# Attention and feed-forward in one kernel: first quad's k and v loaded in three pieces, first batch's q loaded in attention order

## The chip, the cores and the metric

The kernel runs on one core of a Trainium2 chip. The core has five engines that run their own instruction queues in order: TensorE (PE, matmuls; its weight loads are listed as PEld), VectorE (DVE), ScalarE (ACT), GpSimd (POOL) and SyncE (SP), which here issues all the transfers. The metric is the device time of one execution in microseconds (us); the median of three is compared.

## The reference

A linear attention with a feature map, for 8 batches, 8 heads, 576 tokens and head size 64, followed by a feed-forward layer with exact Gelu on its 4608 rows of 512:

```python
def phi(x):
    proj = np.einsum('bhsd,df->bhsf', x, w_phi)
    proj = proj - np.max(np.abs(proj), axis=-1, keepdims=True)
    return np.concatenate([np.exp(proj), np.exp(-proj)], axis=-1)
q_p, k_p = (phi(q), phi(k))
kv = np.einsum('bhsf,bhsd->bhfd', k_p, v)
z = np.sum(k_p, axis=2)
num = np.einsum('bhsf,bhfd->bhsd', q_p, kv)
den = np.einsum('bhsf,bhf->bhs', q_p, z)[..., None] + 1e-06
x = num / den            # then transposed to (tokens, heads * 64)
h = x @ w_in             # 512 to 2048
g = 0.5 * h * (1.0 + erf(h / sqrt(2)))
out = g @ w_out          # 2048 to 512
```

All of it is in float32; w_phi has 128 features.

## The kernel before, in words

**The plan.** The kernel does not issue its instructions as it goes through its loops. Each step is put down as an operation (`Plan.op`, L79) with an engine, an assumed duration, the buffers that it reads and writes, and a rank. `Plan.order` (L105 to L230) then plays the whole kernel through on assumed clocks: at each step it takes, for each engine, the operations that could start first and of those the one with the lowest rank, gives it a start and an end, and frees buffers. `emit` (L232) issues everything in the order of the planned starts. On the chip each engine follows that order and waits by semaphores; the planned times themselves aren't enforced. An operation can be given an earliest planned start with `plan.since`: weight tile n is not loaded before 3.996 x n us (WPACE, L345 and L349), nothing of the feed-forward is planned before TF = 90 us (L622). The plan knows a duration for each kind of operation, hops between engines, TensorE's two clock rates, and a model of the transfers (L204 to L207). It assumes that VectorE and GpSimd do not disturb each other.

**The attention.** `attention(b, rank)` (L519) does a batch: two quads of four heads each. `k_quad` (L366) loads a quad's k (`kt`, 128 x 1152) and v (`vt`, 128 x 18 x 65, the last column ones) with one transfer each (L373, L375), and goes through five units of nine 128-token chunks: projection on TensorE into `pk`, absolute maximum on DVE (`mx`, L404), subtraction on DVE, two exponentials on ACT into `ek` (L408), and sums with v on TensorE into `kv`, copied to `kvn`. `q_pair` (L434) does two heads in two halves of 288 tokens: load `qt` (L443), project into `pq`, copy to `pc` on ACT, absolute maximum over partitions by an all-reduce on POOL (`mb`, L460), subtraction on DVE (`pc`, L311 through a helper), exponentials on ACT (`ef`, L466), and a matmul with `kvn` into `pn`. Results go to DRAM (`x_d`, `d_d`); `quotients` (L508) inverts the denominators. Matmuls are all recorded at L287, elementwise DVE steps at L311, copies at L305.

The operations of batch 0 have ranks from -200 upward in the order in which the code names them. In `q_pair` the load of q, its projection, copy, all-reduce and subtraction of batch 0 get a rank lower by EARLY = 37.5 (L436), so they come ahead of k and v of the same batch. Batch 1 has ranks from -180 (EPACE), the later ones have due times. Some buffers: two each of `kt`, `vt`, `qt`, `pc` and `ef`, one `mb`; the first two batches (EB = 2) use the two `ph` banks for `pq`, `pp` and `po` in turn for `pk`.

**The weights.** `split_weight` (L317) loads each of 32 weight tiles (128 x 512 of 64-bit words, `raw_i` and `raw_o`) and makes two float32r parts of it: one step on ACT, four on DVE (L327 to L333), a cast on ACT, a subtraction on DVE. 

**The feed-forward.** `block` (L539) takes 256 tokens: loads `xr` and `rb` (L552, L556), multiplies and splits them on DVE, and then for eight pairs of 128 columns of the middle layer does matmuls into `ph`, two Gelus on ACT (L582, L583), a subtraction on DVE (`gl`) and matmuls into `po`. There are 18 blocks.

**The start.** A memset on DVE, one small activation, and four matmuls on zeros (`spin`, WARM = 4) stand at the head of TensorE's queue while the first transfers run.

Of the kernel before, what the change touches and what calls it, by code (L numbers as in the profile page):

```python
# [24 lines left out]
NF = 128  # L25
# [29 lines left out]
class Op:  # L55
    __slots__ = ("eng", "cost", "fn", "bufs", "rank", "table", "late", "deps", "users", "wait", "ready", "start", "end", "n", "names", "nbytes", "duty", "kind")


class Plan:
# [18 lines left out]

    def op(self, eng, cost, fn, r=(), w=(), also=(), rank=0.0, table=None, late=0.0, kb=0, duty=1.0, kind="f"):  # L79
        o = Op()  # L80
        o.eng, o.cost, o.fn, o.rank, o.table, o.late, o.n = eng, cost, fn, rank, table, late, len(self.ops)
        o.users, o.ready, o.nbytes, o.duty, o.kind = [], self.since, kb, duty, kind
        deps = set()
        for b in r:
            deps.update(b.writers)
        for b in w:
            deps.update(b.writers)
            deps.update(b.readers)
        for b in r:
# [12 lines left out]
        self.ops.append(o)
        return o

    def order(self, bias):  # L105
# [53 lines left out]
        while len(done) < n:  # L159
# [91 lines left out]
def act(n, psum=False):  # L251
    return (n / 1.2 + (51 if psum else 93)) / 1e3
# [15 lines left out]
def fused_kernel(ctx: ExitStack, tc: tile.TileContext, qT, kT, va, w_st, w_in, w_out, out):  # L268
# [40 lines left out]
    def tt(eng, cost, dst, a, b, o, r, w, **kw):  # L309
        e = {"dve": nc.vector, "pool": nc.gpsimd}[eng]  # L310
        op(eng, cost, lambda: e.tensor_tensor(out=dst(), in0=a(), in1=b(), op=o), r=r, w=w, **kw)  # L311
# [54 lines left out]
    def k_quad(b, g, kvs, rank):  # L366
        def k():
            return dict(rank=next(rank))
# [3 lines left out]
        kt = sb["kt"]([P, KC * P], F32, f"kt_{nm}")  # L372
        op("sp", 0.06, lambda: nc.sync.dma_start(out=kt(), in_=kT[b, g]), w=[kt], kb=590, **k())  # L373
        vt = sb["vt"]([P, 18, D + 1], F32, f"vt_{nm}")
        op("sp", 0.06, lambda: nc.sync.dma_start(out=vt(), in_=va[b, g]), w=[vt], kb=600, **k())  # L375
        kv = [None, None]
# [8 lines left out]
        for u, (p, cs) in enumerate(units):  # L385
            n = len(cs)
            mx = sb["mx"]([P, 2, n], F32, f"mx_{nm}_{u}")
            x = ps[EARLY_PK[turn[0] % len(EARLY_PK)] if b < EB else "pp"]([P, 2, 512], F32, f"pk_{nm}_{u}")
# [10 lines left out]
            def proj(x=x, cs=cs):  # L399
                return [mm(x()[:, j, i * NF : (i + 1) * NF], lhsT=kt()[64 * j : 64 * j + 64, c * P : (c + 1) * P], rhs=wst()[64 * j : 64 * j + 64],  # L400
                           start=True, stop=True) for i, c in enumerate(cs) for j in range(2)]

            op("pe", n * PAIR_K, proj, r=[kt, wst], w=[x], also=[mx, *e], kind="k", **k())
            op("dve", dve(256 * n, True), lambda xs=xs, mx=mx: nc.vector.tensor_reduce(  # L404
                out=mx(), in_=xs(), axis=AX.X, op=ALU.max, apply_absolute_value=True), r=[x], w=[mx], **k())
            tt("dve", dve(256 * n, True), xs, xs, lambda mx=mx, n=n: mx().unsqueeze(3).to_broadcast([P, 2, n, NF]), ALU.subtract, [x, mx], [x], **k())
            for s in (1, 0):
                op("act", act(256 * n, True), lambda xs=xs, es=es, s=s: nc.scalar.activation(  # L408
                    es[s](), xs(), AF.Exp, scale=1.0 - 2.0 * s), r=[x], w=[e[s]], table="exp", **k())
            for pp in (0, 1) if p is None else (p,):  # L410
# [6 lines left out]
                for i, c in enumerate(cs):  # L417
# [10 lines left out]

                    op("pe", 4 * PAIR_V, sums, r=[*e, vt] + ([] if fresh and i == 0 else [acc]), w=[acc], kind="v", **k())
                if last_u:  # L430
# [108 lines left out]
    def block(j, rank):  # L539
# [25 lines left out]
        for u in range(NU):  # L565
# [17 lines left out]
            op("act", act(2 * TB, True) + 0.037, lambda ph=ph: nc.scalar.activation(ph(), ph(), AF.Gelu), r=[ph], w=[ph], table="gelu", rank=URGE + rk)  # L583
            tt("dve", dve(2 * TB, True), gl, ph, lambda gh=gh: gh().bitcast(F32), ALU.subtract, [ph, gh], [gl], rank=URGE + rk)
            for i in range(2):
# [64 lines left out]
LINGER = 3.0  # L650
# [49 lines left out]
```

## Time and profile before

| what | before |
|---|---|
| time, median of three executions | 1153.76 us (1150.57 to 1153.86) |
| the profiled execution's own time | 1153.51 us |
| its span in the trace | 1151.7 us |
| granted TensorE clock, mean of the span | 0.991 of full |
| busy: PE / DVE / ACT / POOL | 1111.6 / 483.5 / 588.9 / 318.2 us |
| TensorE instructions | 9096 matmuls |

How to read it: the profile lists, by engine, how long instructions ran, and for idle time which engine or transfer released it. A timeline row has start and duration in us, the engine, the line, the operation, what it writes and reads, and in brackets the idle time ahead of it with its releaser. In a row of groups the number after the bar is the busy time of the group, then the mean in ns. The chain of work that ended last is followed back from the last instruction. A busy TensorE is not one at its peak, since matmuls are pipelined.

### The profile page before, as it was taken

Reading aid. Unit: us, or ns where it says so; the run is one execution under the profiler, and the core shown is the slowest. Engines: PE = TensorE matmul, PEld = TensorE weight load, DVE = VectorE, ACT = ScalarE, POOL = GpSimd, SP = SyncE. Lnnn points to the kernel's source line nnn. Section 1 sums busy time; section 2 is a strip of 40 time slices with the busy share of each in tenths; the row PEclk is TensorE's granted clock in tenths of the full one; section 3 lists DMA queues with packets and bytes.
Section 4 is the critical chain, followed back from the end, with each engine's and each line's share of the span. In section 5 each row is a group of like instructions: output and inputs, shape, how many; then the busy total and the mean of one; then the engine's idle time right before and its main releaser. Section 6 shows DMA issues by size and latency. Waiting matters only on the chain.

```text
span 1151.7 us, 21761 instructions
## 1 busy us (share of the span) xinstructions
PE 1111.6 (97%) x9096; PEld 914.0 (79%) x9096; DVE 483.5 (42%) x807; ACT 588.9 (51%) x979; POOL 318.2 (28%) x116
## 2 busy tenths in 40 slices
PE   7887899999999999999999999999999999999998
PEld 4544677787787788788878778789898998989997
DVE  5999796344443534444354444432112212122010
ACT  5877586666684776658476675632121222122121
POOL 3323026345452635445263534430000000000000
PEclk8999999999999999999999999999999999999999
DMA  7667631313212041312213121112012021010000
GB/s 264 200 203 239 185 92 53 98 58 108 63 58 83 29 111 34 123 63 70 72 31 113 33 63 37 58 31 56 11 46 55 1 55 39 18 38 19 1 19 19
DMA packets 73939, 84.92 MB, mean 74 GB/s; under 512 B 23968, under 2 KB 60992, under 8 KB 73840
## 3 DMA queue, kind: packets, MB, share of 16 engines
q1 hardware_dynamic: 73840, 83.52, 24.3%
q8 instruction: 71, 1.16, 0.4%
q14 instruction: 28, 0.23, 0.1%
HBM read 64.32 MB, written 19.17 MB: 72 GB/s over the span
## 4 chain that ended last, share of the span: by engine, by line
PE 85%; DVE 7%; DMA 3%; ACT 2%; issue 1%; SPq 1%; POOL 0%; ACTq 0%; DVEq 0%; POOLq 0%
PE po L287 34%; PE ph L287 34%; PE kv L287 6%; PE pn L287 5%; PE pk L287 3%; PE pq L287 3%; DMA dc<-d_d 1%; DVE mx L404 1%; DVE pk L311 1%; DMA vt<-in_va_dram 1%; ACT ek L408 1%; DVE wt_o L331 1%; PE spin L287 1%; DMA x_d<-xo 1%; DVE w_i L311 0%
## 5 line engine op out<-in xcount | busy, mean ns | idle before, releaser
L287 PE MATMUL ph<-xh,w_i 128*128 128x256 f32 x2304 | 429.3, 282 | 0.0
L287 PEld LDWEIGHTS ph<-xh,w_i 128*128 128x128 f32 x2304 | 359.7, 188 | 13.5 <-issue 5.4
L287 PE MATMUL po<-w_o,gh 128*128 128x512 f32 x1152 | 366.9, 400 | 0.0
L287 PE MATMUL ph<-xl,w_i 128*128 128x256 f32 x1152 | 321.2, 279 | 0.0
L311 DVE TENSOR_TENSOR gl<-ph,gh 128x512 fp32r<-128x512 f32 x144 | 99.4, 690 | 386.5 <-ACT ph L583 385.7
L287 PEld LDWEIGHTS po<-w_o,gh 128*128 128x128 f32 x1152 | 207.5, 188 | 56.8 <-issue 9.9
L287 PE MATMUL po<-w_o,gl 128*128 128x512 f32 x576 | 227.8, 395 | 4.2 <-DVE gl L311 4.2
L460 POOL PARTITION_ALL_REDUCE mb<-pc x64 | 142.2, 2222 | 303.6 <-ACT pc L305 258.1
L582 ACT ACTIVATE gh<-ph 128x512 fp32r<-128x512 f32 x144 | 86.3, 599 | 272.6 <-PE ph L287 272.0
L287 PEld LDWEIGHTS ph<-xl,w_i 128*128 128x128 f32 x1152 | 216.5, 188 | 3.3
L495 POOL PARTITION_ALL_REDUCE db<-un x48 | 176.9, 3686 | 140.8 <-DVE un L492 136.5
L287 PEld LDWEIGHTS po<-w_o,gl 128*128 128x128 f32 x576 | 108.4, 188 | 31.1 <-DVE gl L311 5.8
L287 PEld LDWEIGHTS kv<-vt,ek 128*64 128x64 f32 (+1 forms) x2560 | 86.3, 141 | 41.6 <-ACT ek L408 18.0
L287 PE MATMUL pn<-ef,kvn 128*64 128x288 f32 (+1 forms) x512 | 98.8, 427 | 13.2 <-ACT xo L305 13.1
L287 PE MATMUL kv<-vt,ek 128*64 128x65 f32 (+1 forms) x2560 | 98.4, 229 | 13.3 <-ACT ek L408 11.7
L408 ACT ACTIVATE ek<-pk 128x512 f32<-128x512 f32 (+1 forms) x160 | 80.0, 553 | 41.4 <-DVE pk L311 40.6
L466 ACT ACTIVATE ef<-pc 128x576 f32<-128x576 f32 x128 | 83.1, 684 | 24.0 <-DVE pc L311 23.5
L583 ACT ACTIVATE ph<-ph 128x512 f32<-128x512 f32 x144 | 85.5, 594 | 0.0
L311 DVE TENSOR_TENSOR pc<-pc,mb 128x576 f32<-128x576 f32 x64 | 50.5, 790 | 83.1 <-POOL mb L460 83.1
L582 ACT ACT_TABLE_LOAD x55 | 70.6, 1283 | 19.6 <-PE ph L287 18.9
L404 DVE TENSOR_REDUCE mx<-pk 128x4 f32<-128x512 f32 (+1 forms) x80 | 50.5, 633 | 70.9 <-PE pk L287 70.9
L287 PEld LDWEIGHTS pn<-ef,kvn 128*64 128x64 f32 (+1 forms) x512 | 39.3, 138 | 45.4 <-ACT xo L305 17.1
(41 smaller groups left out, 702.3 us busy)
## 6 DMA issues: line engine op xcount, KB each, us to landing
vt<-in_va_dram SPq DMA_DIRECT2D x16, 585.0 KB
qt<-in_qT_dram SPq DMA_DIRECT2D x64, 144.0 KB
kt<-in_kT_dram SPq DMA_DIRECT2D x16, 576.0 KB
out_dram<-ob SPq DMA_DIRECT2D x36, 256.0 KB
raw_i<-in_w_in_dram SPq DMA_DIRECT2D x16, 512.0 KB
raw_o<-in_w_out_dram SPq DMA_DIRECT2D x16, 512.0 KB
x_d<-xo SPq DMA_DIRECT2D x48, 144.0 KB
x_d<-xo SPq DMA_DIRECT2D x32, 72.0 KB
```

Source lines behind the costliest of these rows:

```text
L287: return tc.keep_in_program_order(nc.tensor.matmul(*a, **kw))
L311: op(eng, cost, lambda: e.tensor_tensor(out=dst(), in0=a(), in1=b(), op=o), r=r, w=w, **kw)
L331: op("dve", dve(512), lambda: v.scalar_tensor_tensor(out=t(), in0=low(), scalar=29, in1=t(), op0=ALU.logical_shift_right, op1=ALU.bitwise_ ...
L404: op("dve", dve(256 * n, True), lambda xs=xs, mx=mx: nc.vector.tensor_reduce(out=mx(), in_=xs(), axis=AX.X, op=ALU.max, apply_absolute_val ...
L408: op("act", act(256 * n, True), lambda xs=xs, es=es, s=s: nc.scalar.activation(es[s](), xs(), AF.Exp, scale=1.0 - 2.0 * s), r=[x], w=[e[s] ...
L460: op("pool", 2.2, lambda mb=mb, pc=pc: nc.gpsimd.partition_all_reduce(mb(), pc(), P, bass_isa.ReduceOp.absmax), r=[pc], w=[mb], **k(1))
L466: op("act", act(2 * HS), lambda ef=ef, pc=pc, s=s: nc.scalar.activation(ef()[:, s], pc(), AF.Exp, scale=1.0 - 2.0 * s), r=[pc], w=[ef], ta ...
L495: op("pool", 3.7, lambda db=db, un=un: nc.gpsimd.partition_all_reduce(db(), un(), P, bass_isa.ReduceOp.add), r=[un], w=[db], **k())
L582: op("act", act(2 * TB, True) + 0.016, lambda gh=gh, ph=ph: nc.scalar.activation(gh(), ph(), AF.Gelu), r=[ph], w=[gh], table="gelu", rank= ...
L583: op("act", act(2 * TB, True) + 0.037, lambda ph=ph: nc.scalar.activation(ph(), ph(), AF.Gelu), r=[ph], w=[ph], table="gelu", rank=URGE + rk)
```

## The change

Three things are different in what is built:

1. k and v of batch 0's first quad are each loaded by three transfers (chunks 0 to 1, 2 to 4 and 5 to 8), k and v in turn. Each piece is a buffer of its own to the plan, and a unit's projection and sums depend on the piece that holds their chunks. All other quads keep one transfer each.
2. EARLY goes from 37.5 to 0, so the q steps of batch 0 have their ranks in the order of the code: behind k and v of their quad.
3. The planner charges a VectorE operation 0.9 us more (BLOCKED) where it overlaps a GpSimd operation by more than 0.3 us, once for each GpSimd operation. The operations marked `psum=True` (the maxima and subtractions of k, and the Gelu subtraction) are exempt. No instruction is added by this.

The tile `mx` is twice as wide, and its first half is used. A branch for `b < KB` is never taken, since KB is 0; `plan.since = HOLD2` sets the 0.0 that stood there.

```diff
-    def op(self, eng, cost, fn, r=(), w=(), also=(), rank=0.0, table=None, late=0.0, kb=0, duty=1.0, kind="f"):
+    def op(self, eng, cost, fn, r=(), w=(), also=(), rank=0.0, table=None, late=0.0, kb=0, duty=1.0, kind="f", psum=False):
...
+        taken = []
...
+            if o.eng == "dve" and not o.psum:
+                for span in taken[-4:]:
+                    if t < span[1] - 0.3 and t + cost > span[0] + 0.3 and not span[2]:
+                        span[2] = True
+                        cost += BLOCKED
+            if o.eng == "pool":
+                taken.append([t, t + cost, False])
...
         kt = sb["kt"]([P, KC * P], F32, f"kt_{nm}")
-        op("sp", 0.06, lambda: nc.sync.dma_start(out=kt(), in_=kT[b, g]), w=[kt], kb=590, **k())
         vt = sb["vt"]([P, 18, D + 1], F32, f"vt_{nm}")
-        op("sp", 0.06, lambda: nc.sync.dma_start(out=vt(), in_=va[b, g]), w=[vt], kb=600, **k())
+
+        kp, vp = {}, {}
+        for cut in ((0, 2), (2, 5), (5, KC)) if b == 0 and g < PIECES else ((0, KC),):
+            c0, c1 = cut
+            part, vpart = (Buf(plan, None, None) for _ in range(2))
+            op("sp", 0.06, lambda c0=c0, c1=c1: nc.sync.dma_start(out=kt()[:, c0 * P : c1 * P], in_=kT[b, g, :, c0 * P : c1 * P]),
+               w=[part], also=[kt], kb=65.6 * (c1 - c0), **k())
+            op("sp", 0.06, lambda c0=c0, c1=c1: nc.sync.dma_start(out=vt()[:, 2 * c0 : 2 * c1], in_=va[b, g, :, 2 * c0 : 2 * c1]),
+               w=[vpart], also=[vt], kb=66.6 * (c1 - c0), **k())
+            for c in range(c0, c1):
+                kp[c], vp[c] = part, vpart
...
-            mx = sb["mx"]([P, 2, n], F32, f"mx_{nm}_{u}")
+            mx = sb["mx"]([P, 2, 2 * n], F32, f"mx_{nm}_{u}")
...
-            op("pe", n * PAIR_K, proj, r=[kt, wst], w=[x], also=[mx, *e], kind="k", **k())
+            op("pe", n * PAIR_K, proj, r=[kp[cs[0]], wst], w=[x], also=[kt, mx, *e], kind="k", **k())
...
-                    op("pe", 4 * PAIR_V, sums, r=[*e, vt] + ([] if fresh and i == 0 else [acc]), w=[acc], kind="v", **k())
+                    op("pe", 4 * PAIR_V, sums, r=[*e, vp[c]] + ([] if fresh and i == 0 else [acc]), w=[acc], also=[vt], kind="v", **k())
...
-EARLY = 37.5
+EARLY = 0.0
...
+BLOCKED = 0.9
+HOLD2 = 0.0
...
+KB = 0
...
+PIECES = 1
```

More of the change, by code (lines that the diff above doesn't have):

```diff
@@ L55 @@
 class Op:
-    __slots__ = ("eng", "cost", "fn", "bufs", "rank", "table", "late", "deps", "users", "wait", "ready", "start", "end", "n", "names", "nbytes", "duty", "kind")
+    __slots__ = ("eng", "cost", "fn", "bufs", "rank", "table", "late", "deps", "users", "wait", "ready", "start", "end", "n", "names", "nbytes", "duty", "kind", "psum")
 class Plan:
@@ L77, in pool @@
         return lambda shape, dt, name: Buf(self, tag, lambda: pool.tile(shape, dt, tag=tag, name=name, bufs=bufs))
-    def op(self, eng, cost, fn, r=(), w=(), also=(), rank=0.0, table=None, late=0.0, kb=0, duty=1.0, kind="f"):
+    def op(self, eng, cost, fn, r=(), w=(), also=(), rank=0.0, table=None, late=0.0, kb=0, duty=1.0, kind="f", psum=False):
         o = Op()
         o.eng, o.cost, o.fn, o.rank, o.table, o.late, o.n = eng, cost, fn, rank, table, late, len(self.ops)
-        o.users, o.ready, o.nbytes, o.duty, o.kind = [], self.since, kb, duty, kind
+        o.users, o.ready, o.nbytes, o.duty, o.kind, o.psum = [], self.since, kb, duty, kind, psum
         deps = set()
@@ L401, in proj @@
                            start=True, stop=True) for i, c in enumerate(cs) for j in range(2)]
-            op("pe", n * PAIR_K, proj, r=[kt, wst], w=[x], also=[mx, *e], kind="k", **k())
+            op("pe", n * PAIR_K, proj, r=[kp[cs[0]], wst], w=[x], also=[kt, mx, *e], kind="k", **k())
             op("dve", dve(256 * n, True), lambda xs=xs, mx=mx: nc.vector.tensor_reduce(
-                out=mx(), in_=xs(), axis=AX.X, op=ALU.max, apply_absolute_value=True), r=[x], w=[mx], **k())
-            tt("dve", dve(256 * n, True), xs, xs, lambda mx=mx, n=n: mx().unsqueeze(3).to_broadcast([P, 2, n, NF]), ALU.subtract, [x, mx], [x], **k())
-            for s in (1, 0):
+                out=mx()[:, 0].rearrange("p (j i) -> p j i", j=2), in_=xs(), axis=AX.X, op=ALU.max, apply_absolute_value=True), r=[x], w=[mx], psum=True, **k())
+            if b < KB:
+                op("dve", 0.09, lambda mx=mx: nc.vector.tensor_scalar(
+                    out=mx()[:, 1], in0=mx()[:, 0], scalar1=-1.0, scalar2=None, op0=ALU.mult), r=[mx], w=[mx], **k())
+                for s in (1, 0):
+                    for j in range(2):
+                        for i in range(n):
+                            op("act", act(NF, True), lambda xs=xs, es=es, s=s, j=j, i=i, n=n, mx=mx: nc.scalar.activation(
+                                es[s]()[:, j, i], xs()[:, j, i], AF.Exp, scale=1.0 - 2.0 * s, bias=mx()[:, 1 - s, j * n + i : j * n + i + 1]),
+                               r=[x, mx], w=[e[s]], table="exp", **k())
+            else:
+                tt("dve", dve(256 * n, True), xs, xs, lambda mx=mx, n=n: mx()[:, 0].rearrange("p (j i) -> p j i", j=2).unsqueeze(3).to_broadcast(
+                    [P, 2, n, NF]), ALU.subtract, [x, mx], [x], psum=True, **k())
+            for s in (1, 0) if b >= KB else ():
                 op("act", act(256 * n, True), lambda xs=xs, es=es, s=s: nc.scalar.activation(
@@ L583, in block @@
             op("act", act(2 * TB, True) + 0.037, lambda ph=ph: nc.scalar.activation(ph(), ph(), AF.Gelu), r=[ph], w=[ph], table="gelu", rank=URGE + rk)
-            tt("dve", dve(2 * TB, True), gl, ph, lambda gh=gh: gh().bitcast(F32), ALU.subtract, [ph, gh], [gl], rank=URGE + rk)
+            tt("dve", dve(2 * TB, True), gl, ph, lambda gh=gh: gh().bitcast(F32), ALU.subtract, [ph, gh], [gl], rank=URGE + rk, psum=True)
             for i in range(2):
@@ L619, in fused_kernel @@
             continue
+        plan.since = HOLD2
         r0 = T0 + (b - 1) * AT - LEAD
```

## The prediction

> **What bounds the kernel now.** I read the page first: busy time of each engine, the slices, and the chain that ended last.
>
> ```profile
> span 1151.7 us, 21761 instructions
> PE 1111.6 (97%) x9096; PEld 914.0 (79%) x9096; DVE 483.5 (42%) x807; ACT 588.9 (51%) x979; POOL 318.2 (28%) x116
> PE   7887899999999999999999999999999999999998
> DVE  5999796344443534444354444432112212122010
> PE 85%; DVE 7%; DMA 3%; ACT 2%; issue 1%; SPq 1%; POOL 0%; ACTq 0%; DVEq 0%; POOLq 0%
> ```
>
> TensorE (PE) carries 85% of the chain. Only the first six slices or so, some 180 us, show it below nine tenths, and in those VectorE (DVE) is the busy engine. So I took the view of stretches, 40 us each; its columns are length, busy time of PE, weight load, DVE, ACT and POOL, then the granted clock, DMA share and GB/s.
>
> ```profile
> 0.00:40.00 40.00, 31.58 (x304) 19.59 (x304) 26.09 (x43) 23.81 (x51) 12.79 (x10) 0.91 0.71 246
> 40.00:80.00 40.00, 32.12 (x372) 20.16 (x372) 37.73 (x68) 30.44 (x67) 9.90 (x5) 0.91 0.68 203
> 80.00:120.00 40.00, 30.57 (x327) 18.12 (x324) 36.73 (x58) 32.10 (x71) 14.37 (x6) 0.96 0.75 233
> 120.00:160.00 40.00, 36.21 (x349) 29.65 (x347) 34.94 (x65) 26.88 (x45) 2.14 (x1) 0.99 0.54 152
> 160.00:200.00 40.00, 36.24 (x289) 28.09 (x288) 32.47 (x50) 27.57 (x43) 22.80 (x7) 0.96 0.20 55
> 200.00:240.00 40.00, 40.00 (x380) 32.27 (x378) 16.55 (x28) 27.33 (x42) 17.39 (x7) 1.00 0.28 84
> 320.00:360.00 40.00, 38.55 (x348) 31.51 (x347) 16.94 (x31) 24.10 (x37) 17.16 (x6) 1.00 0.23 64
> 720.00:760.00 40.00, 39.58 (x275) 31.81 (x275) 20.07 (x28) 23.83 (x36) 20.84 (x8) 1.00 0.22 59
> ```
>
> From 200 us on PE has no gap, but for 1.45 us in one of these stretches and 0.42 in another. Before 200 it is idle for 8.42 + 7.88 + 9.43 + 3.79 + 3.76 = 33.3 us. The change leaves the number of matmuls alone, so it can gain only in this head: a microsecond of PE idle that goes there comes off the end, one for one. From 40 to 120 us DVE is busy 74.5 of 80 us (the splitting of weights, and the attention). There an idle or wasted microsecond of DVE is what costs PE.
>
> **Part one, the pieces of k and v.** The start of PE, from its timeline, and the first two stretches of 5 us:
>
> ```profile
> 2.27 6.47 PE L287 MATMUL spin<-idle 128*128 128x512 f32 x8 [2.27 <-ACT idle L292]
> 8.67 0.76 PE L287 MATMUL pq<-qt,wst 64*128 64x288 f32 x4
> 9.26 1.06 PE L287 MATMUL pk<-wst,kt 64*128 64x128 f32 x16
> 10.15 0.81 PE L287 MATMUL pq<-qt,wst 64*128 64x288 f32 x4
> 13.18 2.14 PE L287 MATMUL kv<-vt,ek 128*64 128x65 f32 x64 [2.23 <-ACT ek L408]
> 0.00:5.00 5.00, 2.73 (x4) 1.19 (x5) 0.48 (x1) 1.49 (x2) 0.19 (x4) 1.00 0.55 163
> 5.00:10.00 5.00, 5.00 (x24) 2.57 (x24) 0.09 (x1) 0.55 (x2) 0.00 (x0) 1.00 1.01 392
> ```
>
> The warm-up matmuls (spin) hold PE until 8.74 us, and pq and pk follow with no wait for a transfer. By 5 us 163 x 5 = 815 KB have moved, then 392 KB in each microsecond. In the new order the first quad's k and v (590 + 600 KB in the planner's figures), w_st (66) and two q tiles (2 x 147) are 1550 KB: all landed, as an estimate, at 5 + 735/392 = 6.9 us, before the spin ends. So k in pieces is there earlier and nothing can use it: **gain 0**, whether or not a reader waits for one piece or all three. Four more issues on SP cost nothing as long as the engines of the DMA have work queued, which the share of 1.01 says. Without the cover of the spin, the worth would be the time between the first piece and the last, bounded by 1190/392 = 3.0 us.
>
> The Trainium skill, DMA: Bandwidth & Descriptors, section Bandwidth, speaks against pieces: its table has 138 GB/s for a 64 KB transfer and 341 for 1 MB, and asks for a MiB at a time. By that an estimate for the six pieces, 1190 KB at 138 GB/s, is 8.6 us, q would land after the spin ends, the next part's second term would be lost, and the result would be 1149.6. The trace has transfers of 147 to 600 KB queued back to back at 392 GB/s, which does not bear it out.
>
> **Part two, q in the order of the attention.** Today four pq matmuls go ahead of the first pk. Putting k first starts pk at 8.67 instead of 9.26, and with it the whole DVE stream, by 9.26 - 8.67 = **-0.6 us**; DVE bounds what follows, so I count it whole. Then the DVE and POOL timelines:
>
> ```profile
> 9.91 0.69 DVE L404 TENSOR_REDUCE mx<-pk 128x4 f32<-128x512 f32 x1 [8.53 <-PE pk L287]
> 12.57 0.75 DVE L311 TENSOR_TENSOR pc<-pc,mb 128x576 f32<-128x576 f32 x1
> 15.67 0.76 DVE L311 TENSOR_TENSOR pc<-pc,mb 128x576 f32<-128x576 f32 x1 [2.35 <-POOL mb L460]
> 10.25 2.14 POOL L460 PARTITION_ALL_REDUCE mb<-pc  x1 [9.82 <-ACT pc L305]
> 13.49 2.14 POOL L460 PARTITION_ALL_REDUCE mb<-pc  x1 [1.10 <-DVE pc L311]
> ```
>
> DVE stands still for 2.35 us at 13.3 because the second q subtraction is next in its queue and its all-reduce isn't done; the first quad's later units are behind it. With q after k, units of k fill that place. But the four q halves then come after, each with 2.14 us of all-reduce in front of a DVE instruction, so part of the wait may come back. Bounds 0 and -2.35, and +2.35 if a second such wait arises; I take half, **-1.2 us**, since weight splitting is at hand to fill by then.
>
> **Part three, the planner's new cost.** BLOCKED is the far-reaching edit: the planner now adds 0.9 us, once per POOL instruction, to a DVE instruction on SBUF that overlaps it. No instruction changes, but the order of every queue is worked out anew. Is the charge real? The groups of 0 to 130 us:
>
> ```profile
> L311 DVE TENSOR_TENSOR w_i<-wt_i,w_i 128x512 fp32r<-128x512 f32 x12 | 10.6, 880 | 1.6 <-ACT w_i L305 1.4
> L331 DVE SCALAR_TENSOR_TENSOR wt_i<-raw_i,wt_i 128x512 uint32<-128x512 uint32 x12 | 9.2, 770 | 0.2
> L333 DVE SCALAR_TENSOR_TENSOR wt_o<-raw_o,wt_o 128x512 uint32<-128x512 uint32 x11 | 8.4, 771 | 0.1
> L311 DVE TENSOR_TENSOR w_o<-wt_o,w_o 128x512 fp32r<-128x512 f32 x10 | 8.1, 829 | 1.5 <-ACT w_o L305 1.5
> L331 DVE SCALAR_TENSOR_TENSOR wt_o<-raw_o,wt_o 128x512 uint32<-128x512 uint32 x11 | 7.4, 684 | 0.1
> L327 DVE TENSOR_SCALAR wt_o<-wt_o 128x512 f32<-128x512 f32 x11 | 7.3, 671 | 0.2 <-ACT wt_o L326 0.2
> L329 DVE TENSOR_SCALAR wt_i<-wt_i 128x512 uint32<-128x512 uint32 x12 | 5.0, 422 | 0.1
> ```
>
> Against 684 ns for the same tile with two inputs and 422 with one, the others are long by 12 x 0.196 + 12 x 0.086 + 11 x 0.087 + 10 x 0.145 + 11 x 0.249 = 8.5 us, over the 16 all-reduces of two batches: about half a microsecond each that today's plan doesn't know of. The plan must then run ahead of the chip, and SP's timeline shows it where the code pins a plan time:
>
> ```profile
> 38.62 0.36 SPq L323 DMA_DIRECT2D raw_i<-in_w_in_dram  x1
> 67.35 0.36 SPq L323 DMA_DIRECT2D raw_o<-in_w_out_dram  x1
> 101.12 1.30 SPq L552 DMA_DIRECT2D xr<-x_d  x1
> 106.56 0.60 SPq L323 DMA_DIRECT2D raw_i<-in_w_in_dram  x1
> ```
>
> Counted from 0, these are weight loads 9, 15 and 24, and the first load of the feed-forward. The plan pins them at 3.996 x n or later and at TF = 90, so 36.0, 59.9, 95.9 and 90.0: the chip is late by 2.7, 7.4, 10.7 and 11.1 us. With some 16 x 0.9 = 14.4 us charged at most, the new plan keeps pace or lags a little, so weights and feed-forward loads stand some 10 us earlier in the queues against the attention of batches 1 and 2. What PE could gain from feed-forward work 10 us earlier:
>
> ```profile
> 116.04 1.19 PE L287 MATMUL pn<-ef,kvn 128*65 128x288 f32 x4 [2.92 <-ACT xo L305]
> 117.59 1.13 PE L287 MATMUL kv<-vt,ek 128*64 128x65 f32 x16 [0.37 <-ACT ek L408]
> 123.86 0.49 PE L287 MATMUL ph<-xh,w_i 128*128 128x256 f32 x1
> ```
>
> The first ph would start near 114 instead of 123.86 and fill these two gaps: 2.92 + 0.37 = **-3.3 us**. Bounds: nothing if DVE, being full, only trades one kind of work for another; at best these and the 7.55 us that PE idles from 120 to 200, -10.8 us; and above nothing, +5.9, the third rival's price. I take the gaps, the row where the moved work lands. After 200 us a new order has 1.87 us to win and as much to lose as it likes; I count 0.
>
> **The sum.** 0 - 0.6 - 1.2 - 3.3 = -5.1 us. The profiled execution took 1153.51 us (span 1151.7, 1.8 around it), 0.25 below the median of 1153.76; 1153.5 - 5.1 = **1148.4 us**. A measurement of this kernel tells about 0.3%, 3.5 us, from no change, so this would be seen as faster.
>
> **Rivals.** *Nothing to see:* DVE at 37.73 and 36.73 of 40 us is full whatever the order, so earlier feed-forward work takes its DVE time from the attention, PE loses there what it gains, and the waits for all-reduces come back. Only the earlier start stays: 1153.5 - 0.6 = 1152.9. For it speaks that the DVE work is the same to the instruction; against it, that a feed-forward group gives PE far more work for each DVE instruction than a weight or k does.
>
> *Slower, weights before attention:* the 10.7 us of lateness at load 24 are 10.7/4.0 = 2.7 weight tiles that the new plan puts ahead of attention work. A tile takes DVE 2 x 0.42 + 3 x 0.69 = 2.9 us, so attention is put off by 7.8 us of DVE, while no feed-forward matmul is ready before about 114. PE, busy 30.57 of 40 us then, loses 7.8 x 0.76 = 5.9 us: 1153.5 - 0.6 + 5.9 = 1158.8. It decides if PE's idle time from 40 to 120 us, now 17.3, comes to over 20. For it: T0, LEAD and WPACE stay as they were for the old plan. Against: the attention of batches 0 and 1 has the lower ranks, and the weights get what it leaves.
>
> *The change doesn't do what it says:* if the pieces only landed together, nothing would differ, as part one found.
>
> **The numbers.** Forecast (1142.7 to 1150.2, from the terms' far ends: all of the gaps and 5 us of the idle time behind them) 0.50; nothing to see 0.28; slower 0.22, of which about half lies within 4 us of no change. The range that leaves out 2 in 10: 1142 to 1157.5. Faster by over 0.3% 0.50, within 0.28, slower 0.22.
>
> **What would show it.** Part one: the spin still ends at 8.7, pk starts right behind it, kt and vt unwaited for. Part two: first DVE reduce near 9.3, no 2.35 us wait for mb before 16. Part three: weight load 24 near 97 to 100, the first xr load near 91 to 93, first ph near 114, PE idle before 200 us at 28 instead of 33.3. It is wrong if the first ph comes earlier and the idle total stays (first rival), if PE idles over 20 us from 40 to 120 (second), or if gaps open after 200 us.

## The result and the profile after

The changed kernel took 1161.62 us (median of 6, 1158.80 to 1164.28), the kernel before, on the same chip, 1153.33 us (median of 6, 1149.72 to 1153.90). The ratio is 1.0067, with a 95% interval of 1.0047 to 1.0087: slower by about two thirds of a per cent, where I forecast a gain of 5 us. The profiled execution took 1164.28 us (span 1162.5, mean granted clock 0.987 of full).

From the page of the changed kernel, the same lines as of before (span, busy time, slices of PE and of DVE, the chain by engine):

```profile
span 1162.5 us, 21746 instructions
PE 1121.1 (96%) x9096; PEld 921.7 (79%) x9096; DVE 503.8 (43%) x807; ACT 590.3 (51%) x981; POOL 320.0 (28%) x116
PE   8887898999999999999999999999999999999998
DVE  6997799353554535334543546352212112121110
PE 80%; DVE 8%; ACT 4%; DMA 3%; POOL 2%; issue 2%; SPq 1%; ACTq 0%; DVEq 0%; POOLq 0%
```

The second line holds the surprise. PE executes the same 9096 matmuls and is busy for 1121.1 us instead of 1111.6. So of the 10.8 us by which the span grew, 9.5 are matmuls that take longer, and 1.3 are idle time of PE (1162.5 - 1121.1 = 41.4 us against 40.1). Of the 9.5, 2.4 fall in the first 200 us (PE busy 169.2 us against 166.7), the other 7.1 behind them. The stretches of 40 us in the changed kernel:

```profile
0.00:40.00 40.00, 33.23 (x382) 21.05 (x382) 28.52 (x48) 27.43 (x60) 11.68 (x9) 0.96 0.78 264
40.00:80.00 40.00, 33.15 (x407) 20.83 (x405) 37.14 (x62) 31.20 (x69) 13.35 (x6) 0.96 0.76 228
80.00:120.00 40.00, 31.18 (x273) 18.18 (x274) 31.46 (x52) 26.38 (x59) 11.40 (x5) 0.91 0.71 200
120.00:160.00 40.00, 35.78 (x316) 29.69 (x315) 33.81 (x59) 26.30 (x42) 5.11 (x2) 0.91 0.54 157
160.00:200.00 40.00, 35.81 (x269) 28.25 (x269) 39.38 (x61) 24.07 (x40) 20.15 (x5) 0.91 0.15 41
```

Before 200 us PE is idle for 6.77 + 6.85 + 8.82 + 4.22 + 4.19 = 30.9 us, 2.4 less than before; summed in the same way over the 23 stretches from 200 to 1120 us it is idle for 6.2 us instead of 1.9. The rest is in the durations. The group view (busy time, mean in ns of one, idle time ahead) of the matmuls of the feed-forward's first layer, before and after:

```profile
L287 PE MATMUL ph<-xh,w_i 128*128 128x256 f32 x2304 | 429.3, 282 | 0.0
L287 PE MATMUL ph<-xl,w_i 128*128 128x256 f32 x1152 | 321.2, 279 | 0.0
```

```profile
L295 PE MATMUL ph<-xh,w_i 128*128 128x256 f32 x2304 | 437.9, 284 | 0.1
L295 PE MATMUL ph<-xl,w_i 128*128 128x256 f32 x1152 | 324.3, 281 | 0.0
```

Each lasts 2 ns longer, and there are 3456 of them. The timeline shows it as a rhythm, here in a late block in which nothing else stands between them. Each row is two matmuls with xh, and one with xl follows, so seven rows hold six triples. Before, then after:

```profile
1048.10 0.39 PE L287 MATMUL ph<-xh,w_i 128*128 128x256 f32 x2
...
1050.14 0.39 PE L287 MATMUL ph<-xh,w_i 128*128 128x256 f32 x2
```

```profile
1048.15 0.40 PE L295 MATMUL ph<-xh,w_i 128*128 128x256 f32 x2
...
1050.27 0.40 PE L295 MATMUL ph<-xh,w_i 128*128 128x256 f32 x2
```

18 matmuls take 2.04 us before and 2.12 us after. Over all of the last eight blocks, from the starts of consecutive weight loads in the trace (steps of over 200 ns left out), it is 116.0 ns a matmul before and 118.1 after, at a granted clock of 1.00 in both.

### The profile page after: what moved, and what is told of

Same layout as the page of the kernel before. It is cut to its first block, busy times and chain, and to the rows that moved or that the text cites. A ratio compares the mean times of both kernels' runs of the same rounds, so it can differ in the third digit from the quotient of the medians.

```text
span 1162.5 us, 21746 instructions
## 1 busy us (share of the span) xinstructions
PE 1121.1 (96%) x9096; PEld 921.7 (79%) x9096; DVE 503.8 (43%) x807; ACT 590.3 (51%) x981; POOL 320.0 (28%) x116
## 4 chain that ended last, share of the span: by engine, by line
PE 80%; DVE 8%; ACT 4%; DMA 3%; POOL 2%; issue 2%; SPq 1%; ACTq 0%; DVEq 0%; POOLq 0%
PE po L295 33%; PE ph L295 32%; PE kv L295 5%; PE pn L295 5%; PE pk L295 3%; PE pq L295 2%; POOL mb L489 1%; DVE pc L319 1%; DMA dc<-d_d 1%; DMA raw_i<-in_w_in_dram 1%; DVE wt_o L339 1%; DVE wt_i L341 1%; ACT ek L437 1%; DVE pk L319 1%; DMA x_d<-xo 1%
## 5 line engine op out<-in xcount | busy, mean ns | idle before, releaser
L295 PE MATMUL ph<-xh,w_i 128*128 128x256 f32 x2304 | 437.9, 284 | 0.1
L295 PEld LDWEIGHTS ph<-xh,w_i 128*128 128x128 f32 x2304 | 363.9, 189 | 15.5 <-issue 7.0
L295 PE MATMUL kv<-vt,ek 128*64 128x65 f32 (+1 forms) x2560 | 98.0, 227 | 13.4 <-ACT ek L437 12.4
L319 DVE TENSOR_TENSOR pc<-pc,mb 128x576 f32<-128x576 f32 x64 | 57.4, 897 | 76.4 <-POOL mb L489 76.4
```

What stands on the lines that cost most here:

```text
L295: return tc.keep_in_program_order(nc.tensor.matmul(*a, **kw))
```

## The experiments

There are two questions: why the same matmuls became slower, and what each of the three edits does. For the first, the start addresses in the built kernels were the key. A tile gets its place in SBUF when the first instruction that uses it is issued, one tile behind another. A new order of the queues therefore moves the buffers. The first tile of xl (low part of x, the moving operand of a third of the ph matmuls) starts at byte 87936 of a partition before, 128 above a multiple of 256; in the changed kernel it starts at 88064, which is a multiple of 256. Of the operands of ph, nothing else changed its offset modulo 256: w_i lies at 64 and 128, 0, 192 and 192 for its four quarters, xh at 128. Of the other buffers, qt, pc, mb and one tile of w_o changed theirs.

Kernels that did not run side by side are compared by their ratio to the kernel before that ran beside each. Diffs are against the changed kernel, but for the one run that is a changed kernel before.

| run | what it has | us | before, beside it | ratio, 95% interval |
|---|---|---|---|---|
| e1 | pieces | 1158.78 | 1153.59 | 1.0047 (1.0033 to 1.0061) |
| e2 | q order | 1159.32 | 1153.59 | 1.0055 (1.0041 to 1.0069) |
| e3 | charge | 1148.04 | 1153.59 | 0.9953 (0.9938 to 0.9967) |
| e4 | pieces, q order | 1159.40 | 1153.59 | 1.0053 (1.0037 to 1.0068) |
| e5 | all three, xl put back | 1157.84 | 1153.69 | 1.0034 (1.0021 to 1.0046) |
| e6 | none, xl moved | 1159.11 | 1153.69 | 1.0046 (1.0028 to 1.0063) |
| e7 | charge, w_i at 192 | 1143.95 | 1153.69 | 0.9911 (0.9891 to 0.9931) |
| e8 | as e7, gl and w_o moved too | 1151.06 | 1153.69 | 0.9980 (0.9966 to 0.9994) |
| e9 | pieces, charge; places as before | 1151.70 | 1153.42 | 0.9990 (0.9971 to 1.0009) |
| e10 | q order, charge; places as before | 1156.10 | 1153.42 | 1.0021 (1.0008 to 1.0033) |
| e11 | pieces, q order; places as before | 1154.87 | 1153.42 | 1.0003 (0.9989 to 1.0018) |
| e12 | all three, w_i at 192 | 1151.28 | 1153.42 | 0.9986 (0.9972 to 1.0000) |
| e13 | all three, places as before, third xo | 1153.88 | 1154.73 | 0.9997 (0.9985 to 1.0010) |
| e14 | as e7, third xo | 1140.01 | 1154.73 | 0.9880 (0.9860 to 0.9900) |
| e15 | as e7, gl moved; one execution | 1145.32 | 1154.73 | |
| e16 | as e7, w_o moved; one execution | 1141.95 | 1154.73 | |
| e17 | as e7, xl moved; one execution | 1155.15 | 1156.92 | |

**One edit at a time.** The theories at this point were that the planner's new charge, the q order, or any new order at all against constants tuned for the old one carries the loss.

e1, the pieces alone:

```diff
-EARLY = 0.0
+EARLY = 37.5
-BLOCKED = 0.9
+BLOCKED = 0.0
```

> Only the pieces of k and v; EARLY stays 37.5 and nothing is charged for GpSimd. Theory A (the planner's new cost carries the loss, since it brings feed-forward and weight loads forward): 1153.3, no change. Theory B (q behind k carries it): 1153.3 as well. Theory C (the constants fit one order of the queues, and any new order costs some us, whatever edit makes it): 1153 to 1158, as far as the order of the queues changes. The prediction's part one says 0.

e2, the order of q alone:

```diff
-BLOCKED = 0.9
+BLOCKED = 0.0
-PIECES = 1
+PIECES = 0
```

> Only q in the order of the attention (EARLY 0). Theory A: 1151 to 1154. Theory B: 1158 to 1162, with DVE waiting for the all-reduce more than 2.35 us in the first 30 us. Theory C: some us off 1153.3, to either side.

e3, the charge alone:

```diff
-EARLY = 0.0
+EARLY = 37.5
-PIECES = 1
+PIECES = 0
```

> Only the planner's charge of 0.9 us (BLOCKED). Theory A: 1159 to 1163, the first feed-forward load near 92 instead of 101 us and a wait of PE for the store of x_d near 100 us. Theory B: 1151 to 1154. Theory C: some us off 1153.3, not adding up with the other two to the whole.

e4, pieces and q order:

```diff
-BLOCKED = 0.9
+BLOCKED = 0.0
```

> Pieces and q order, without the charge (BLOCKED 0). Theory A: 1151 to 1154, that is 7 to 10 us better than the whole change. Theory B: 1159 to 1163, like the whole change. Theory C: neither; a sum that does not follow from the parts.

The charge alone gains 5.5 us. The pieces alone lose 5.2, the q order alone 5.7, and both together 5.8: losses that are the same and don't add are not the price of two edits. What the three losers share with the changed kernel is the place of xl, a multiple of 256 in all of them and at 128 in e3. They also share 118 ns a ph matmul, against 116.0 in e3.

**The place alone.** An unused tile ahead of the first use of a tag moves what comes behind it and leaves every queue in its order:

```diff
+        def make(shape, dt, name):
+            n = PADS.pop(tag, 0)
+            if n:
+                pool.tile([P, n // 4], F32, tag=f"pad_{tag}", name=f"pad_{tag}", bufs=1)
+            return pool.tile(shape, dt, tag=tag, name=name, bufs=bufs)
```

e5, the changed kernel with xl (and w_o behind it) put back:

```diff
+PADS = {"xl": 128, "w_o2": 128}
```

> The whole change with two unused gaps of 128 bytes in SBUF, so that xl and one w_o tile have the offsets modulo 256 that they have before the change; not one instruction and no order differs from the whole change. Theory L (the change moves buffers, and the ph matmuls run some 2 ns slower each where xl starts at a multiple of 256 bytes): ph matmuls back at 116 ns apart, 3456 x 2 ns = 7 us less, 1153 to 1156. Theory C (the order of the queues costs it): 1161.6, as the whole change.

e6, the kernel before with xl, and nothing else, moved to a multiple of 256:

```diff
+PADS = {"xl": 128, "kvn": 128}
```

> The kernel before, every queue in its order, with two unused gaps of 128 bytes, so that xl alone starts at a multiple of 256 bytes. Theory L: 1158 to 1161, with ph matmuls 118 ns apart all through the run. Theory C: 1153.3, no change.

e6 settles the first question. No instruction, order or dependency is different from the kernel before, and it is slower by 5.4 us. The busy time of PE on its page (1111.6 before) grew by 5.3 of them:

```profile
PE 1116.9 (97%) x9096; PEld 921.9 (80%) x9096; DVE 484.6 (42%) x807; ACT 588.3 (51%) x979; POOL 317.7 (27%) x116
```

In the last eight blocks the loss lies in the second half of each, whose quarters of w_i lie at 192: there a ph matmul goes from 113.6 to 117.8 ns. In the first half, with w_i at 64, 128 and 0, it takes 118.4 ns before and 118.3 with xl moved.

e5 has PE busy for 1111.4 us, as before, and gets only 3.8 of the 8.3 us back: a second cause remains.

**Better places.** Since the half of a block with w_i at 192 is the faster one in the kernel before, I placed all of w_i at 192, and then gl and w_o of the second layer too, at 192 and 128 (gh lies at 192 in all kernels).

e7 (with the charge alone):

```diff
+PADS = {"w_i0_0": 128, "w_i3_0": 192, "xh": 192, "w_i0_1": 192, "w_o4": 64}
```

> The planner's charge alone, with gaps that put all w_i tiles at 192 modulo 256 and xh and xl at 128, the offsets at which the second half of each block's ph matmuls is 113 to 114 ns apart before. Theory L, if the offsets of weight and moving tile are all that counts: the first half falls from 118.5 to 113.5, 1728 x 5 ns = 8.6 us less than the charge alone (1148.0), 1139 to 1141. Theory C: 1148.

e8:

```diff
+PADS = {"gl": 64, "w_i0_0": 64, "w_i3_0": 192, "xh": 192, "w_o2": 128, "w_i0_1": 64, "w_o4": 192, "w_i0_2": 128, "w_o8": 192, "w_i0_3": 64, "w_o12": 192, "gh": 64, "w_o14": 192}
```

> As the run before, and the second layer's matmuls laid out by the same rule (gh and gl at 192, w_o at 128). If that rule holds for them too, po matmuls fall from about 232 ns to 225 or so, 1728 x 7 ns = 12 us more, about 1128; if the rule does not carry over, 1137 to 1143.

e7 gained 4.1 us more over e3 and beats both kernels, at 113.7 ns a ph matmul in the late blocks. e8 lost this gain again, and more: its ph matmuls went to 117.8 ns though their own operands lie as in e7. (xr, rb and some buffers of the attention moved along with gl and w_o.)

**What the parts do at equal places.** For the second cause I repeated the pairs with every buffer at the offset modulo 256 that it has before (in e12 all but w_i and the raw tiles that share its places).

e9 (pieces and charge):

```diff
-EARLY = 0.0
+EARLY = 37.5
+PADS = {'xl': 128, 'xo': 128}
```

> The loads in pieces and the charge of 0.9 us, q in the old order; unused tiles of 128 bytes a partition ahead of xl and xo give each buffer the offset modulo 256 bytes that it has in the kernel before. Theory L (placement, and the rest adds up): 1148.0 of the charge alone and nothing from the pieces, whose loss of 5 us in the first run was the place of xl: 1147 to 1149. Theory I (the parts clash with each other in the order of the work, since the changed kernel with xl moved back still took 1157.8): if it is the pieces that clash with the charge, 1154 to 1158.

e10 (q order and charge):

```diff
-PIECES = 1
+PIECES = 0
+PADS = {'qt': 64, 'w_i0_0': 192, 'pc': 192, 'xh': 64, 'mb': 192, 'ob': 64, 'xl': 128, 'xo': 128, 'w_o1': 128, 'w_o2': 128}
```

> The first batch's q in the order of the attention and the charge of 0.9 us, k and v in one piece; the offsets modulo 256 bytes are those of the kernel before. Theory L with parts that add up: 1147 to 1149. Theory I: if it is the order of q that clashes with the charge, 1154 to 1158, with a wait of TensorE for a store of the attention's output near 100 us, as in the changed kernel, and more than 5 us of idle time after 200 us; the better of this run and the one with pieces and charge tells which of the two is at fault, and if both are at 1148 it takes all three.

e11 (pieces and q order):

```diff
-BLOCKED = 0.9
+BLOCKED = 0.0
+PADS = {'qt': 64, 'w_i0_0': 192, 'pc': 192, 'xh': 64, 'mb': 192, 'ob': 64, 'xl': 128, 'xo': 128, 'w_o1': 128, 'w_o2': 128}
```

> The pieces and the new order of q without the charge, as in an earlier run that took 1159.4, now with the offsets modulo 256 bytes of the kernel before. Theory L: the 5.4 us that moving xl alone cost come back, so 1153 to 1155, about the kernel before (1153.7). A theory by which the new order of the queues itself costs the time: 1158 to 1160 as in that run.

e12 (the changed kernel with all of w_i at 192):

```diff
+PADS = {'qt': 64, 'w_i0_0': 64, 'mx': 128, 'pc': 192, 'xh': 64, 'w_i3_0': 64, 'mb': 128, 'ob': 64, 'xl': 128, 'xo': 128, 'w_o1': 128, 'w_o2': 128, 'w_i0_1': 192, 'w_o4': 64}
```

> The changed kernel, its order untouched, with every tile of w_i at 192 and xh and xl at 128 bytes modulo 256, all other buffers as in the kernel before. Theory L: the same placement took 4.1 us off the kernel with the charge alone, so 1157.8 less 4.1: 1152 to 1155, and weight loads of ph about 113.7 ns apart. If that earlier gain had another cause than the places of w_i, xh and xl: 1157 to 1159.

e11 is the same as before (1.0003), which 1.0053 was with xl moved: pieces and q order together are neutral, and their whole loss was the place. e12 repeats the gain of e7 in another order, 1.0034 to 0.9986. But the charge, worth -0.5% on the old order, is worth nothing or less on the others: 0.9990 with pieces, 1.0021 with the q order, 1.0034 with both against 1.0003 without it. The parts clash, as Theory I had it: they don't add up, and the q order does most of it.

**Where it clashes.** The records of the changed kernel show a stop of PE at 100 us. The chain of waits, then the rows of ACT and PE:

```profile
97.97 7.52 DMA x_d<-xo
105.55 0.40 ACT xo L313
```

```profile
105.55 0.39 ACT L313 COPY xo<-pn 65x288 f32<-65x288 f32 x1 [6.67 <-DMA x_d<-xo]
106.00 2.18 PE L295 MATMUL pn<-ef,kvn 128*65 128x288 f32 x4 [5.68 <-ACT xo L313]
```

A store of the attention's output took 7.52 us to land, behind loads that SP had issued ahead of it (weights at 90.82 and 94.84 us, x for the feed-forward at 92.65 and 96.04); one of the two xo buffers waited for it, ACT for the buffer, PE for ACT. Would a third buffer give the time back? The order isn't planned with it.

e13 (all three parts, places as before):

```diff
+            return pool.tile(shape, dt, tag=tag, name=name, bufs=3 if tag == "xo" else bufs)
+PADS = {'qt': 64, 'w_i0_0': 192, 'pc': 192, 'xh': 64, 'mb': 192, 'ob': 64, 'xl': 128, 'xo': 128, 'w_o2': 128}
```

> The changed kernel in its own order, buffers at the offsets modulo 256 bytes of the kernel before, and a third buffer for the attention's output xo, which the order isn't planned with. Theory S (the stop near 106 us behind the slow store carries the loss): the wait of 5.7 us goes, 1157.8 less 3 to 5.7, so 1152 to 1155, with the first ph some 4 us earlier. Theory R (what is late next takes its place, since weights 24 to 31 set the first ph anyway, and the rest of the loss is idle time after 200 us): 1156.5 to 1158.5, with the wait gone from its row and another in its place.

e14 (the charge alone, places as e7):

```diff
+            return pool.tile(shape, dt, tag=tag, name=name, bufs=3 if tag == "xo" else bufs)
+PADS = {'w_i0_0': 128, 'pc': 128, 'w_i3_0': 64, 'xh': 192, 'w_o3': 128, 'w_i0_1': 192, 'w_o4': 64}
```

> The charge alone with the old order of q and one piece, every tile of w_i at 192 and xh and xl at 128 bytes modulo 256 (1143.95 in an earlier run), with a third buffer for xo. Waits for xo of that order stand at 7.1 us in the rows, of which one long one is not known: Theory S 1140 to 1143; Theory R 1143 to 1145.

Both gained about the same, 1.0034 (e5) to 0.9997 and 0.9911 (e7) to 0.9880, so Theory S holds as to the buffer and falls as to the clash: the wait for xo costs nearly as much where nothing clashes. (e13 also puts qt, pc and mb where before has them, and e14 moves pc, mb and mx; no operand of ph or po lies elsewhere within either pair.) The groups of pn, with the idle time ahead of them, in e5 and e13, then in e7 and e14:

```profile
L302 PE MATMUL pn<-ef,kvn 128*65 128x288 f32 x128 | 40.1, 435 | 13.7 <-ACT xo L320 10.1 <-ACT ef L502 3.4
```

```profile
L302 PE MATMUL pn<-ef,kvn 128*65 128x288 f32 x128 | 40.5, 438 | 11.0 <-ACT xo L320 7.3 <-ACT ef L502 3.6
```

```profile
L302 PE MATMUL pn<-ef,kvn 128*65 128x288 f32 x128 | 39.3, 430 | 8.6 <-ACT xo L320 7.9 <-ACT ef L502 0.4
```

```profile
L302 PE MATMUL pn<-ef,kvn 128*65 128x288 f32 x128 | 39.1, 428 | 5.9 <-ACT xo L320 5.3 <-ACT ef L502 0.4
```

The wait shrank by 2.8 us in the one order and by 2.6 in the other. In the kernel before it is 12.2 us, more than in the order that clashes. e14, at 1140.01 us, is the fastest of all.

**Which places matter.** One execution each, so the busy time of PE is what I compare: from e7, gl alone, w_o alone, xl alone. Some buffers of the attention (pc, mb, mx and one of ek) lie elsewhere modulo 256 than in e7. They lie so in e14 too, whose ph matmuls take the same 113.7 ns.

e15 (gl from 128 to 192):

```diff
+PADS = {'gl': 64, 'qt': 192, 'w_i0_0': 128, 'pc': 128, 'w_i3_0': 64, 'xh': 192, 'w_i0_1': 192, 'w_o4': 64}
```

> As the run with w_i at 192 and xh and xl at 128 bytes modulo 256, with gl alone moved from 128 to 192. If gl's place is what gave that gain back in the run with gh, gl and w_o moved too: ph weight loads 117 to 118 ns apart in the late blocks and TensorE busy 1113 to 1115 us. If it is w_o's: 113.7 ns and 1106 to 1108 us.

e16 (w_o to 128):

```diff
+PADS = {'w_i0_0': 128, 'pc': 128, 'w_i3_0': 64, 'xh': 192, 'w_o2': 128, 'xo': 128, 'w_o3': 128, 'w_i0_1': 64, 'w_o4': 192, 'dc': 128, 'w_o8': 192, 'xr': 64, 'w_o11': 192, 'w_i0_3': 64, 'w_o12': 192, 'gh': 64, 'w_o14': 192, 'un': 64}
```

> As the run with w_i at 192 and xh and xl at 128 bytes modulo 256, with every tile of w_o moved to 128. If w_o's place is what gave the gain back: TensorE busy 1113 to 1115 us, ph weight loads 117 to 118 ns apart in the late blocks. If it is gl's: 113.7 ns and 1106 to 1108 us.

e17 (xl from 128 to 0):

```diff
+PADS = {'w_i0_0': 128, 'pc': 128, 'w_i3_0': 64, 'xh': 192, 'xl': 128, 'kvn': 128, 'w_i0_1': 192, 'w_o4': 64}
```

> As the run with every tile of w_i at 192 and xh and xl at 128 bytes modulo 256, with xl alone moved to 0. If xl at 0 costs by itself: ph weight loads 2 ns further apart than 113.7, about 115.7, and TensorE busy 1112 to 1114 us. If the rate hangs on the whole arrangement, another number: 113.3 to 114, busy 1104 to 1108, or the 117.7 that the move of gl gave.

The PE lines of the pages of e7, e15, e16 and e17, in this order:

```profile
PE 1106.5 (97%) x9096; PEld 910.2 (80%) x9096; DVE 489.4 (43%) x807; ACT 594.2 (52%) x985; POOL 320.2 (28%) x116
```

```profile
PE 1107.2 (97%) x9096; PEld 914.1 (80%) x9096; DVE 491.4 (43%) x807; ACT 594.5 (52%) x985; POOL 321.1 (28%) x116
```

```profile
PE 1103.1 (97%) x9096; PEld 907.2 (80%) x9096; DVE 491.5 (43%) x807; ACT 595.1 (52%) x985; POOL 320.0 (28%) x116
```

```profile
PE 1119.9 (97%) x9096; PEld 922.4 (80%) x9096; DVE 491.2 (43%) x807; ACT 595.2 (52%) x985; POOL 318.5 (28%) x116
```

xl at a multiple of 256 costs PE 13.4 us here, twice and a half what it cost in e6, and ph goes from 113.7 to 117.8 ns in the last eight blocks. In e6 only the half of the matmuls with w_i at 192 had a faster pace to lose, here all of them. So the two bad places don't add: with w_i at 64, 128 or 0, with xl at 0, or with both, a ph matmul takes about 118 ns. w_o at 128 does no harm (113.3 ns). gl, which no ph matmul reads, brings ph to 117.7 ns, as e8 had it, but in the last eight blocks alone: in the first ten ph takes 115.5 ns in e15, 114.9 in e7 and 117.5 in e17. The second layer's matmuls (po) come 228.7 ns apart in the late blocks of e15 instead of 232.4 in e7, an even 226 to 227 in the second half of a block, and PE's busy time hardly moves. Both expectations for e15 were half right: gl's place is what set ph in the late blocks of e8, and it alone does not give the time back.

## Why the prediction was wrong, point by point

**What failed first** is a step that I took without an argument, in the first part: the change leaves the number of matmuls alone, "so it can gain only in this head", and after 200 us "I count 0". It assumes that a matmul's duration is not touched by an order. 3456 matmuls at 118.1 instead of 116.0 ns are 7 us, worked out for all of them, and a measured 5.4 in e6 and, between e11 and e4, 5.8 (0.5% of 1153.6). No rival held it either. The Trainium skill would not have warned me: TensorE: Matmul & The Clock Gate, section Back-to-back issue gap, gives the spacing of matmuls by the number of columns only, about 81 ns for 128 and 131 for 512 in a stream of weight loads and matmuls, and 262 cycles for 256 for a matmul by itself. At that page's 2.4 GHz the last is an estimate of 109 ns. The 113.3 to 118.1 ns of these runs lie between its figures for a stream, but they differ for one and the same form, by the place of the buffers.

**Part one, the pieces.** Right as to the time. The rows of the start of the changed kernel:

```profile
2.27 5.51 PE L295 MATMUL spin<-idle 128*128 128x512 f32 x8 [2.27 <-ACT idle L300]
7.71 0.97 PEld L295 LDWEIGHTS pk<-wst,kt 64*128 64x128 f32 x16 [0.76 <-DMA qt<-in_qT_dram]
7.71 1.16 PE L295 MATMUL pk<-wst,kt 64*128 64x128 f32 x16
8.47 0.69 DVE L421 TENSOR_REDUCE mx<-pk 128x4 f32<-128x512 f32 x1 [7.09 <-PE pk L295]
12.75 0.42 DVE L421 TENSOR_REDUCE mx<-pk 128x2 f32<-128x256 f32 x1 [1.53 <-PE pk L295]
14.96 0.75 DVE L319 TENSOR_TENSOR pc<-pc,mb 128x576 f32<-128x576 f32 x1
```

pk follows the spin without a gap, and PE waited for no transfer of k or v. (The 0.76 us ahead of pk's first weight load are put down to a transfer of q, which pk doesn't read; ahead of the first load in the kernel before stand 0.78 us of issue.) By the landings in the trace the pieces of k were in at 3.7, 4.6 and 7.0 us, those of v at 4.1, 5.6 and 7.8, and the two q tiles at 8.2 and 8.5, so all was in later than the 6.9 that I had estimated. From the first issue at 1.18 us to the last landing of v the six pieces took 6.6 us. The estimate for them from the Trainium skill, DMA: Bandwidth & Descriptors, section Bandwidth, was 8.6 us. q landed behind the end of the spin at 7.78, but pq stands behind pk and started at 8.70, so this cost nothing that the run shows. At equal place of xl, e1 (1.0047) is as e6 (1.0046), so the gain of 0 stands.

**Part two, the order of q.** The signs came, but the larger one was luck: the first maximum is at 8.47 us instead of 9.91 mostly because the spin took 5.51 us instead of 6.47 in this execution. In e5, with the same queues, the spin took 6.72 us and the first maximum came at 9.68. Counted from the end of the spin it is 0.69 us instead of 1.17, a gain of 0.5 us where I said 0.6. There is no wait of 2.35 us for mb. But the -1.8 us did not come off the end. e2 at 1.0055 is no better than e6 at 1.0046 with the same place of xl, and e11 has PE idle for 35.9 us before 200 us, where before has 33.3. That DVE's start "bounds what follows, so I count it whole" is the step that fell: a wait of 1.53 us for pk stands in the rows above already, and the idle time of PE did not fall.

**Part three, the charge.** The mechanism was right and its size too small on the order that I argued from: -3.3 forecast, -5.5 in e3, within the bounds that I gave. Before 200 us PE idles for 27.3 us in e3 instead of 33.3. What is charged is real, too: in the kernel before, four of the sixteen subtractions for w_i on DVE last 1.38 to 1.63 us, each wholly within an all-reduce of POOL, and the others 0.68 to 0.69; the Gelu subtractions, which are exempt, last 0.69 us with an all-reduce beside them or without. In the changed kernel the marks of this step are near where I put them:

```profile
92.65 0.33 SPq L581 DMA_DIRECT2D xr<-x_d  x1
99.73 0.45 SPq L331 DMA_DIRECT2D raw_i<-in_w_in_dram  x1
116.94 0.49 PE L295 MATMUL ph<-xh,w_i 128*128 128x256 f32 x1
```

First load of the feed-forward at 92.65 (91 to 93 said), weight load 24 at 99.73 (97 to 100), first ph at 116.94, 6.9 us earlier than before (I said 114). What fell is that this is worth the same with the other two edits. Six kernels with xl at 128 and ph at 116.0 ns show how it goes (idle time of PE and busy time of DVE in us, from the view of stretches and the page of each; DVE has 807 instructions in all of them):

| run | what it has | ratio | PE idle, 0 to 200 us | 200 to 1120 us | DVE busy |
|---|---|---|---|---|---|
| before | none | 1 | 33.3 | 1.9 | 483.5 |
| e11 | pieces, q order | 1.0003 | 35.9 | 2.5 | 485.6 |
| e3 | charge | 0.9953 | 27.3 | 4.3 | 491.4 |
| e9 | pieces, charge | 0.9990 | 26.2 | 6.2 | 493.4 |
| e10 | q order, charge | 1.0021 | 31.9 | 7.1 | 503.8 |
| e5 | all three | 1.0034 | 32.3 | 6.5 | 504.0 |

On the old order the charge takes 6.0 us off the idle time before 200 us and adds 2.4 behind it. With the other two edits (e11 to e5) it takes off 3.6 and adds 4.0, so nothing is left. So the "I count 0" for the time after 200 us fell here too, by idle time. DVE's busy time goes along: the charge makes the plan count what DVE loses beside POOL, it doesn't keep the two apart, and with the q order the same 807 instructions take 18 to 20 us longer than without the charge. That this makes the gaps is not shown; no run changed it alone.

Where the idle time before 200 us stands differs from order to order. Three stretches of 10 us, in the changed kernel and then in e3 (after PE, PEld, DVE, ACT and POOL come granted clock, DMA share and GB/s):

```profile
100.00:110.00 10.00, 3.84 (x11) 1.53 (x8) 4.50 (x8) 4.02 (x9) 2.25 (x2) 0.75 0.83 209
130.00:140.00 10.00, 7.50 (x57) 6.46 (x58) 9.59 (x20) 6.52 (x12) 0.00 (x0) 0.66 0.46 152
180.00:190.00 10.00, 6.48 (x26) 5.17 (x25) 10.00 (x17) 9.33 (x15) 2.61 (x2) 0.67 0.16 37
```

```profile
100.00:110.00 10.00, 6.57 (x60) 3.46 (x60) 8.32 (x12) 6.71 (x15) 6.22 (x3) 0.99 1.03 312
130.00:140.00 10.00, 10.00 (x115) 8.53 (x115) 9.73 (x19) 7.11 (x11) 0.00 (x0) 1.00 0.63 201
180.00:190.00 10.00, 9.68 (x96) 8.01 (x95) 10.00 (x18) 8.48 (x13) 3.47 (x1) 1.00 0.05 15
```

The changed kernel loses 2.5 to 6.2 us of PE in each of the three, most of it in single stops, and the clock is 0.66 to 0.75 in the same stretches. e3 loses 3.43 us in the first and almost nothing in the other two, but it has a stop of its own elsewhere:

```profile
160.00:170.00 10.00, 6.15 (x30) 4.48 (x32) 10.00 (x16) 4.59 (x7) 3.63 (x1) 1.00 0.04 16
```

So single stops don't tell the orders apart; the sums in the table do. Of low clocks e3 has one from 100 us on, 0.67 in the stretch from 110 to 120. Over the first 200 us PE idles for 30.9 us in the changed kernel and for 27.3 in e3, and the part of the clock that was not granted comes to 14.0 us (0.04, 0.04, 0.09, 0.09 and 0.09 of 40 us) against 8.8. Some of this differs from one execution to the next: in e5, with the queues of the changed kernel, it is 10.8. The Trainium skill, TensorE: Matmul & The Clock Gate, section What's actually happening, has the clock halved after an idle window of about 3.4 us. The stop of 5.68 us agrees; the one of 3.19 us at 180 is a little shorter than that and has the low clock behind it all the same. So has one of 2.91 us in e3, which ends at 110.59. The stop at 180, from ACT and PE:

```profile
179.91 0.62 ACT L313 CAST w_o<-wt_o 128x512 fp32r<-128x512 f32 x1 [4.56 <-DVE wt_o L341]
181.14 0.68 ACT L495 ACTIVATE ef<-pc 128x576 f32<-128x576 f32 x1 [0.62 <-DVE pc L319]
181.84 1.28 ACT L611 ACT_TABLE_LOAD   x1
183.14 0.60 ACT L611 ACTIVATE gh<-ph 128x512 fp32r<-128x512 f32 x1
183.79 1.22 PE L295 MATMUL po<-w_o,gh 128*128 128x512 f32 x2 [3.19 <-ACT gh L611]
```

A weight's cast stood ahead of a Gelu in ACT's queue and waited 4.56 us for DVE, which was busy without a gap; behind it an exponential waited 0.62 us more for DVE, and the table for Gelu took 1.28 us to load. PE waited for the Gelu. e10, with the q order and the charge, has all three stretches in the same way (4.23, 8.22 and 6.38 us of PE, clocks of 0.74, 0.66 and 0.83). That these stops are the clash is read from the records and not shown by a run: the third buffer shortened the first stop (to 3.81 us in e13) and gained as much in the order that has no clash. Why the charge puts its gaps where it does only with the q order stays open; no run tried to take the q order's loads or that cast out of the way.

**The rivals.** The one on the slower side gave 1158.8, near the measured time, by a way that did not happen: from 40 to 120 us PE idles for 15.7 us (6.85 + 8.82), not over 20. A number that is right for the wrong reason would have taught the wrong thing. What I had named as a sign of being wrong, "if gaps open after 200 us", came true: 6.2 us for 1.9. Nearest by its mechanism is "nothing to see": the first ph came 6.9 us earlier, and PE's idle time over the whole span stayed (41.4 us for 40.1; 43.1 in e5). The lower end of the forecast was added up wrongly: the far ends that it names, 0.6, 2.35, 3.3 and 5 us, give 1142.3, and 1142.7 is the best case of part three alone.

**The sum as measured.** By ratios, the changed kernel lost 0.67%. 0.33% is the place of xl (e5), and 0.34% remains, where the charge (-0.47%) and the neutral other two should have left a gain: a clash of 0.8%, some 9 us.

## What to carry to other kernels

Look at the busy time of the bounding engine before its idle time: if the same instructions take longer, no wait explains the difference. An edit that changes the order in which buffers are first used changes where they lie, so compare the start addresses of matmul operands before giving a small difference to the edit, and make a control that moves a buffer and nothing else. And test the parts of a replanned change together and not only one by one: here a charge that gained 0.5% alone gained nothing with parts that were neutral.

## What the runs showed of the hardware that I had not expected

The pace of matmuls on the same shapes, at full clock, hangs on where the buffers lie in a partition. In the last eight blocks a ph matmul took 113.3 to 113.7 ns with w_i at 192 and xh and xl at 128 modulo 256 bytes, 116.0 with w_i mixed, and 117.8 to 118.1 with xl at 0, whether w_i was at 192 or mixed. A shift of xl by 128 bytes makes the difference; kernels in which it is shifted by 256, 1024 or 4352 from its place in before (e5, e11 and e9) have the 116.0 of before. It is not a matter of an operand's own place alone: moving gl, which ph doesn't read, took ph from 113.7 to 117.7 ns in the blocks in which nothing else stands between the matmuls, and made po an even 226 to 227 ns in half of each of them. What sets it was not found out. Moving buffers and a third buffer for xo took the kernel with the charge from 1148.04 us to 1140.01 in e14 (0.9953 to 0.9880 of before) with not one instruction put in another place.
